# Retiming a hand-written scheduler: longer exponential rounds in the plan, a hold on TensorE, shorter key-value runs

## The chip, the cores and the metric

One core of a Trainium2 chip. The metric is the device time of one execution in microseconds, as the median of several runs. The engines are TensorE (PE; its weight loads are PEld), VectorE (DVE), ScalarE (ACT), GpSimd (POOL) and SyncE (SP).

## The reference

Four residual layers on x of 2048 rows by 512, each on a layer-normed x: A, B, A, B.

```python
def _A_ref(x, wq, wk, wv, wo):          # 32 query heads of 16, one key head, one value head
    q = (x @ wq).reshape(B, S, H, Dh).transpose(0, 2, 1, 3)
    k = x @ wk
    v = x @ wv
    scores = jnp.einsum("bhqd,bkd->bhqk", q, k) * (Dh ** -0.5)
    o = jnp.einsum("bhqk,bkd->bhqd", softmax(scores), v)
    return o.transpose(0, 2, 1, 3).reshape(B, S, H * Dh) @ wo

def _B_ref(x, wqkv, wo):                # linear attention, 32 heads of 16
    q, k, v = ...                       # x @ wqkv, split
    phi = lambda t: jnp.where(t > 0, t + 1, jnp.exp(t)) + 1e-6
    pq, pk = phi(q), phi(k)
    kv = jnp.einsum("bhsd,bhse->bhde", pk, v)
    z = jnp.einsum("bhsd->bhd", pk)
    num = jnp.einsum("bhqd,bhde->bhqe", pq, kv)
    den = jnp.einsum("bhqd,bhd->bhq", pq, z)[..., None] + 1e-6
    return (num / den).transpose(0, 2, 1, 3).reshape(B, S, D) @ wo

for _ in range(2):
    x = x + _A_ref(layernorm(x), A_wq, A_wk, A_wv, A_wo)
    x = x + _B_ref(layernorm(x), B_wqkv, B_wo)
```

## The kernel before

The program's layers are L = 0 to 3; 0 and 2 are softmax attention (`run_a`), 1 and 3 linear attention (`run_b`). The sequence is cut into 16 tiles of 128 rows. In an attention layer a score block is 128 keys by 512 columns (128 queries of 4 heads), so a layer has 4096/2 = 2048 blocks. TensorE makes the scores of several blocks at once in separate row strips (L937); the exponential of a block is made either on ScalarE, 1 to 3 blocks in one ACTIVATE (L1118, a round), or on VectorE, where one eviction to an integer form (L1205) and three shifted copies of up to four blocks (L1247) approximate it. TensorE then sums exponentials times values in column strips into bank 6 (L991), with `V` for ScalarE's blocks and four weighted copies `VW` for VectorE's. PSUM's banks 0 to 5 form two sets of score banks, bases 0 and 3; ScalarE's rounds alternate between them. While one set is read by a round, the other is filled by TensorE.

Nothing of the order on an engine is written out by hand. When the kernel is built, a discrete-event planner (`Planner`) runs generators for all tiles and layers. Each operation has a duration and a latency, given as numbers in the source, and a priority; a free engine takes the ready operation of the best priority (`_dispatch1`). The order so found is written as five fixed instruction streams with semaphore waits (`emit`). The chip keeps these orders and has its own times. The numbers that matter here:

- an exponential round of n blocks lasts 0.051 + 0.4267 n us in the plan (L1118), and its result is there `EX_LAT` = 0.185 later;
- scores take `QK_DUR` = 0.22, are there after `QK_LAT` = 0.438, and a change of TensorE's mode (row strips, column strips, full) costs `SWITCH` = 0.107; scores have priority 0.0, weighted sums 2.0;
- when TensorE has nothing ready, `fill` (L1017 to L1039) issues dummy matmuls of 128 to 512 columns (L1036), as far as a budget allows that grows by `WORK` columns per 3.413 us, and no longer than up to the next expected end of a round (`pl.due`, L1120);
- `soon` (L62) holds an operation back when a better one is about to be ready within `LAG`, but only while `calm`, which is outside the stretches of exponentials;
- `alone` (L1215) gives VectorE a block of its own when its planned backlog is under `DXB`.

In linear layers, `kvt` (layer 3) and `kv_` (layer 1) sum pk times v of a group of 3 or 4 tiles on TensorE, as one operation per bank: 12 or 16 matmuls that the planner treats as one indivisible piece (L1490 to L1502, L1627 to L1636). Most of a linear layer's work is spread among the rounds of the attention layer before or after it; between the last scores of layer 0 and the first of layer 2 lies a short stretch without exponentials, here called the seam.

Of the kernel before, what the change touches and what calls it, by code (L numbers as in the profile page):

```python
# [35 lines left out]
class Planner:  # L36
# [3 lines left out]
    def __init__(self, nc):  # L40
        self.nc = nc
        self.now = 0.0
        self.events = []
        self.seq = 0
        self.ready = {e: [] for e in ENGS}
        self.busy = {e: False for e in ENGS}
        self.until = {e: 0.0 for e in ENGS}
        self.order = {e: [] for e in ENGS}
        self.writer = {}
        self.readers = {}  # L50
        self.flags = {}
        self.flagwait = {}
        self.level = (0.0, 0.0)
        self.due = []
        self.idle = []
        self.mode = None
        self.port = 0.0
        self.calm = False
        self.hungry = []
        self.near = {e: [] for e in ENGS}  # L60

    def soon(self, e, o, dur):  # L62
        lag = {DV: LAG, AC: LAG, PE: LAGP}.get(e)
        if not self.calm or lag is None:
            return 0.0
        n = self.near[e] = [x for x in self.near[e] if x[0] > self.now and x[2].eng is None]
        t = [x[0] for x in n if x[1] + 0.3 < o.prio and x[0] + lag < self.now + dur]
        return min(t) if t else 0.0

    def at(self, t, fn):  # L70
        self.seq += 1
# [68 lines left out]

    def _dispatch(self, e):
        self._dispatch1(e)
        if e == PE and not self.busy[e] and self.idle:
            self.due = [t for t in self.due if t > self.now]
            for f in self.idle:
                f()
        if e == DV and self.hungry and (not self.ready[DV] or self.backlog(DV) < DXB):
            self.hungry[0]()

    def _dispatch1(self, e):  # L150
        if self.busy[e]:
            return
        h = self.ready[e]
        held = []
        while h:
            x = heapq.heappop(h)
            o = x[2]
            if o.eng is not None:
                continue
            dur, fn = o.opts[e]  # L160
            if o.port and self.port > self.now:
                held.append(x)
                continue
            w = self.soon(e, o, dur)
            if w:
                held.append(x)
                self.at(w, lambda: self._dispatch(e))
                break
            if e == PE and STICK and o.mode != "row" and o.mode != self.mode != "row":
                like = [y for y in h if y[2].eng is None and y[2].mode == self.mode and y[0] <= o.prio + STICK]  # L170
                if like:
                    y = min(like)
                    h.remove(y)
                    heapq.heapify(h)
                    held.append(x)
                    o = y[2]
                    dur, fn = o.opts[e]
            if o.port:
                self.port = self.now + dur
            if e == PE:  # L180
                if self.mode != o.mode:
                    dur += max(SWITCH - (self.now - self.until[e]), ROWIN if o.mode == "row" else 0.0)
                self.mode = o.mode
            if e == PE and self.now < COLD:
                dur *= 1.9
            o.eng, o.fn = e, fn
            self.order[e].append(o)
# [190 lines left out]
SWITCH = 0.107  # L378
ROWIN = 0.025
PV_LAT = 0.215  # L380
EX_LAT = 0.185
DH_DUR = 0.22
AH_DUR = 0.28
NBQ = 3
LAG = 0.15
LAGP = 0.05
QLATE = {1: range(4, 14), 3: ()}
PQ = ()
# [1 line left out]
LNEXP = 6  # L390
MCRIT = {0: (), 1: (0, 1), 2: (), 3: ()}
ECRIT = (15,)
WORK = 5000
RING = 24
NOB = 4
DTL = 3.6
# [7 lines left out]
GROW = (5,)  # L404
BLS = 1.6
BLO = 5.0
DXB = 1.6
BLT = 2.5
GA = 3
MW = [None, None, 0, 1, 2, 2, 2, 3, 4, 5, 6, 7, 8, 9, 10, 11]  # L410
# [45 lines left out]
DG = [[0]] + [[t, t + 1] for t in range(1, 15, 2)] + [[15]]  # L456
ACRS = True
EB = "rs"
MCOP = (DV,)*4
EVP = 1.2  # L460
DPP = 1.5
# [7 lines left out]
def bass_interleave_layers__grouped_kv_mqa__linear_attn_block__prompt_kernel(  # L469
# [124 lines left out]
    def B_(i):  # L594
        return ("bank", i)
# [332 lines left out]
    def run_a(L):  # L928
# [111 lines left out]

        pl.idle.append(fill)

        def act_stream():
            if CLM[L]:
                yield ("flag", CLM[L])
# [9 lines left out]
            pl.calm = False  # L1055
            while True:
                s_ = yield ("acq", sets, 0.0)
                group = []
                split = None
                while len(group) < size[s_] and split is None and state["si"] < len(segs):  # L1060
# [54 lines left out]
                if chunk["blk"] and stale():  # L1115
                    dve_close()
                p_ = yield ("acq", pt_pool, 0.0)
                ex = op({AC: (0.051 + 0.4267 * n, lambda e, n=n, s_=s_, p_=p_: e.activation(PT[:, p_, 0:n * 512], ps[:, s_ * 512:(s_ + n) * 512], ACTF.Exp, scale=EXPSC, bias=EXPBIAS))},  # L1118
                        writes=bk + [("PT", p_)], prio=1.0, lat=EX_LAT)
                ex.begun = lambda n=n: pl.due.append(pl.now + 0.051 + 0.4267 * n + 0.17)  # L1120
                pl.give_after(sets, s_, [ex] if split is None else [ex, p1])
                pv_post(ex, [(sg, kt, j, PT[:, p_, i * 512:(i + 1) * 512], ("PT", p_)) for i, (sg, kt, j) in enumerate(group)], [n, [], pt_pool, p_])
            state["done"] = lin["done"] = True
# [76 lines left out]
        def dve_take(extra, own):  # L1200
            sg, kt, j, b = extra
            h, f_ = len(chunk["blk"]), chunk["f"]
            chunk["blk"].append((sg, kt, j))
            dst = FB[:, f_, h * 512:(h + 1) * 512]
            o = op({DV: (0.602, lambda e: e.tensor_scalar(out=dst.bitcast(I16), in0=bank(b), scalar1=VB, scalar2=VLO, op0=ALU.add, op1=ALU.max))},  # L1205
                   writes=[B_(b), ("FB", f_, h)], prio=2.0 if own else 0.5, lat=0.15)
# [164 lines left out]
    def run_b(L):  # L1371
# [93 lines left out]
        def kvt(gi, ts):  # L1465
# [19 lines left out]
            for i, (c, n) in ((1, parts[1]), (0, parts[0])):  # L1485
# [1 line left out]
                    bs[i] = yield ("acq", banks, pr)  # L1487
                b = bs[i]

                def fn(e, i=i, b=b):  # L1490
                    ins = None
                    for g in range(4):
                        for t in ts:
                            if i:
                                ins = e.matmul(ps[:, b * 512 + g:b * 512 + g + 1], lhsT=pk[:, t % 8, g * P:(g + 1) * P], rhs=va[:, t % 8, H * 17 - 1:H * 17],
# [3 lines left out]
                                               start=(not end and t == ts[0]), stop=(t == ts[-1]), skip_group_check=True)  # L1499
                    return ins  # L1500
                rd = [("pk", t % 8) for t in ts] + [("va", t % 8) for t in ts] + [("sacc", u) for u in sorted({2 + t % 8 // 2 for t in ts})]
                op({PE: ((0.04 if i else 0.07) * 4 * len(ts), fn)}, reads=rd, writes=[B_(b)], prio=pr, lat=0.2).cols = (16 if i else 512) * len(ts)  # L1502
                dst = kvacc[:, c:c + n]
                if end:
                    continue
# [94 lines left out]
        def kv_(gi, ts):  # L1600
# [19 lines left out]
            for gs in ((0, 1, 2), (3,)):  # L1620
# [3 lines left out]
                else:  # L1624
                    b = yield ("acq", banks, pr)

                def fn(e, gs=gs, b=b):  # L1627
                    ins = None
                    for i, g in enumerate(gs):
                        for t in ts:  # L1630
                            ins = e.matmul(ps[:, b * 512 + i * 136:b * 512 + (i + 1) * 136], lhsT=pk[:, t % 8, g * P:(g + 1) * P],
                                           rhs=va[:, t % 8, g * 136:(g + 1) * 136], start=(not end and t == ts[0]), stop=(t == ts[-1]), skip_group_check=True)
                    return ins
                rd = [("pk", t % 8) for t in ts] + [("va", t % 8) for t in ts] + [("sacc", u) for u in sorted({2 + t % 8 // 2 for t in ts})]
                o = op({PE: (0.08 * len(gs) * len(ts), fn)}, reads=rd, writes=[B_(b)], prio=pr, lat=0.2)
                o.cols = 136 * len(gs) * len(ts)  # L1636
                dst = kvacc[:, gs[0] * 136:gs[0] * 136 + n]
                if end:
                    continue
# [200 lines left out]
```

## Time and profile before

| | |
|---|---|
| median of 3 runs | 1493.02 us (1491.22 to 1494.28) |
| the profiled execution | 1491.74 us, its span 1490.0 us |
| granted TensorE clock | 0.999 |
| PE busy | 1401.7 us (94%) |
| DVE busy | 1440.6 us (97%) |
| ACT busy | 1455.6 us (98%) |
| exponential rounds (L1118) | 1309, 1399.7 us busy |
| VectorE's evictions (L1205), shifts (L1247) | 1046, 688.9 us; 786, 516.5 us |

A busy engine's records can overlap, so the sum of the means is more than its busy time. A PE that is busy by its records can still be waiting between them.

### The profile page before, as it was taken

How to read it: one execution, taken by the hardware profiler on the slowest of the kernel's cores; microseconds unless marked ns; L12 is line 12 of the kernel's file. 1: busy time of each engine (PE TensorE's matmuls, PEld its weight loads, DVE VectorE, ACT ScalarE, POOL GpSimd, SP SyncE). 2: the span in 40 equal slices, each digit the busy share in tenths (PEclk: the TensorE clock that was granted, in tenths of full speed). 3: DMA queues.
4: the chain of work that ended last, by engine and by line, in shares of the span. 5: the costliest groups of instructions: out<-in, count | busy, mean ns of one | idle time of the engine just before them, and what ended most of it. 6: DMA issues, size and time to landing. Idle time of an engine off the chain costs nothing.

```text
span 1490.0 us, 36100 instructions
## 1 busy us (share of the span) xinstructions
PE 1401.7 (94%) x14660; PEld 511.8 (34%) x14755; DVE 1440.6 (97%) x2684; ACT 1455.6 (98%) x1442; POOL 76.9 (5%) x155
## 2 busy tenths in 40 slices
PE   8999999999999999999999999999999999999998
PEld 4423333322323333323743333333333333333335
DVE  7899999999999999999879999999999999999997
ACT  8999999999999999999799999999999999999996
POOL 5000000000000000000022000000000000000000
PEclk9999999999999999999999999999999999999999
DMA  5100000000000000000031000000000000000001
GB/s 117 71 9 8 9 8 6 8 5 8 9 9 9 9 5 5 2 1 2 2 47 40 2 12 9 12 8 9 4 9 5 9 9 9 8 2 1 2 2 58
DMA packets 53540, 20.71 MB, mean 14 GB/s; under 512 B 47232, under 2 KB 52864, under 8 KB 53376
## 3 DMA queue, kind: packets, MB, share of 16 engines
q1 hardware_dynamic: 52320, 18.36, 5.7%
q8 instruction: 118, 1.93, 0.5%
q14 instruction: 46, 0.38, 0.1%
q10 hardware_dynamic: 1056, 0.03, 0.0%
HBM read 5.28 MB, written 2.10 MB: 5 GB/s over the span
## 4 chain that ended last, share of the span: by engine, by line
DVE 17%; PE 16%; ACT 12%; issue 5%; DMA 1%; ACTq 0%
ACT PT L1118 12%; DVE FB L1205 7%; DVE FB L1247 6%; PE ps L991 5%; PE ps L937 5%; PE ps L683 2%; PE ps L1036 1%; PE ps L851 1%; PE ps L1292 1%; DMA xnT<-xn 1%; DVE sacc L1270 0%; ACT phE L1377 0%; DVE st L765 0%; PE ps L922 0%; DVE QT L1380 0%
## 5 line engine op out<-in xcount | busy, mean ns | idle before, releaser
L1118 ACT ACTIVATE PT<-ps 128x1024 bf16<-128x1024 f32 (+1 forms) x1309 | 1399.7, 1224 | 4.6 <-PE ps L937 3.4
L1205 DVE TENSOR_SCALAR FB<-ps 128x512 int16<-128x512 f32 x1046 | 688.9, 681 | 6.9 <-PE ps L937 4.6
L937 PE MATMUL ps<-QT,KM 32*128 32x512 bf16 x4096 | 530.2, 385 | 36.9 <-ACT PT L1118 23.8
L991 PE MATMUL ps<-FB,VW 128*32 128x512 bf16 x4184 | 527.9, 385 | 17.4 <-ACT PT L1118 6.3
L1247 DVE TENSOR_SCALAR FB<-FB 128x2048 int16<-128x2048 int16 x786 | 516.5, 679 | 0.4
L991 PE MATMUL ps<-PT,V 128*32 128x512 bf16 x3050 | 482.8, 386 | 13.4 <-ACT PT L1118 9.9
L937 PEld LDWEIGHTS ps<-QT,KM 32*128 32x128 bf16 x4096 | 133.0, 91 | 433.7 <-ACT PT L1118 301.2
L991 PEld LDWEIGHTS ps<-FB,VW 128*32 128x32 bf16 x4184 | 131.8, 94 | 184.4 <-issue 83.5
L1036 PE MATMUL ps<-QT,V 128*32 128x512 bf16 (+6 forms) x758 | 178.4, 312 | 1.6 <-DVE FB L1205 1.6
L991 PEld LDWEIGHTS ps<-PT,V 128*32 128x32 bf16 x3050 | 120.6, 94 | 128.6 <-issue 59.9
L1036 PEld LDWEIGHTS ps<-QT,V 128*32 128x32 bf16 x758 | 60.0, 95 | 81.5 <-issue 52.0
L756 POOL TENSOR_TENSOR rs<-ve,mhalf 128x1 f32<-128x1 f32 x59 | 43.5, 738 | 579.7 <-DVE ve L754 576.6
L683 PE MATMUL ps<-wqkv,xnT 128*128 128x512 bf16 (+1 forms) x220 | 62.8, 367 | 5.7 <-issue 3.2
L754 POOL TENSOR_SCALAR ve<-mv 128x1 f32<-128x1 f32 x32 | 14.1, 439 | 674.3 <-DVE mv L766 674.1
L1377 ACT ACTIVATE phE<-ps 128x512 bf16<-128x512 f32 (+1 forms) x66 | 42.0, 638 | 6.2 <-PE ps L851 4.6
L1292 PE MATMUL ps<-identF,sacc 128*128 128x128 f32 x256 | 46.8, 291 | 0.8 <-DVE sacc L1270 0.8
L1270 DVE COPY sacc<-ps 128x512 f32<-128x512 f32 x64 | 43.6, 681 | 1.3 <-PE ps L991 1.1
L765 DVE BATCH_NORM_STATS2 st<-x_sb 128x6 f32<-128x512 bf16 x60 | 40.6, 681 | 2.2 <-DMA x_sb<-in_A_x_dram 2.0
L851 PE MATMUL ps<-xnT,wqkv 128*128 128x128 bf16 x512 | 38.8, 220 | 0.0
L851 PE MATMUL ps<-xnT,wq 128*128 128x128 bf16 x464 | 36.3, 220 | 0.9 <-DVE FB L1205 0.4
L1292 PEld LDWEIGHTS ps<-identF,sacc 128*128 128x128 f32 x256 | 27.4, 140 | 22.2 <-issue 13.5
L851 PEld LDWEIGHTS ps<-xnT,wqkv 128*128 128x128 bf16 x512 | 29.7, 98 | 10.0 <-issue 6.6
(139 smaller groups left out, 630.9 us busy)
## 6 DMA issues: line engine op xcount, KB each, us to landing
out_dram<-x_sb SPq DMA_DIRECT2D x16, 128.0 KB, 1.7
x_sb<-in_A_x_dram SPq DMA_DIRECT2D x6, 256.0 KB, 4.4
wqkv<-in_B_wqkv_dram SPq DMA_DIRECT2D x1, 1536.0 KB, 8.8
xnT<-xn SPq DMA_TRANSPOSE x48, 2.4
x_sb<-in_A_x_dram SPq DMA_DIRECT2D x4, 128.0 KB, 2.2
wq<-in_A_wq_dram SPq DMA_DIRECT2D x1, 512.0 KB, 4.2
wo<-in_A_wo_dram SPq DMA_DIRECT2D x1, 512.0 KB, 4.0
wo<-in_B_wo_dram SPq DMA_DIRECT2D x1, 512.0 KB, 9.6
```

The source lines that it names most:

```text
L683: return e.matmul(dst, lhsT=l, rhs=r, start=(k == 0), stop=(k == len(pairs) - 1))
L756: op({PO: (0.55, lambda e: e.tensor_tensor(out=rs[:, t:t + 1], in0=ve[:, t:t + 1], in1=mhalf[:], op=ALU.pow))}, reads=[("ve", t), "mhalf"] ...
L851: ins = e.matmul(dst[:, g * P:(g + 1) * P], lhsT=lhs(g, k), rhs=rhs(k), start=(k == 0), stop=(k == FT - 1))
L937: return e.matmul(bank(b), lhsT=KM[r, sg.par, kt * P:(kt + 1) * P], rhs=QT[r, sg.t, :], start=True, stop=True)
L991: ins = e.matmul(ps[32 * j:32 * j + 32, ACC * 512:(ACC + 1) * 512], lhsT=V[:, kt, :] if w is None else VW[:, kt, w, :], rhs=ap, start=(k = ...
L1036: o = op({PE: (n / 2400.0, lambda e: e.matmul(ps[32 * j:32 * j + 32, b * 512:b * 512 + n], lhsT=V0[:], rhs=QT[:, sg.t, 0:n], start=st, sto ...
L1118: ex = op({AC: (0.051 + 0.4267 * n, lambda e, n=n, s_=s_, p_=p_: e.activation(PT[:, p_, 0:n * 512], ps[:, s_ * 512:(s_ + n) * 512], ACTF.E ...
L1205: o = op({DV: (0.602, lambda e: e.tensor_scalar(out=dst.bitcast(I16), in0=bank(b), scalar1=VB, scalar2=VLO, op0=ALU.add, op1=ALU.max))}, w ...
L1247: o = op({en: (du, lambda e, w=w, g_=g_: e.tensor_scalar(out=FB[:, g_, 0:n].bitcast(I16), in0=FB[:, f_, 0:n].bitcast(I16), scalar1=float(w ...
L1270: o = op({DV: (0.6, lambda e, src=src: e.tensor_copy(src, bank(ACC)))}, writes=[B_(ACC), key], prio=0.0, lat=0.15)
L1292: o = op({PE: (0.12, lambda e, c=c: e.transpose(ps[:, b * 512 + c * P:b * 512 + (c + 1) * P], src[:, c * P:(c + 1) * P], identF[:]))}, rea ...
L1377: op({AC: (0.07 + n / 1200.0, lambda e: e.activation(phE[:, i, 0:n], bank(b, n), ACTF.Exp))}, reads=[B_(b)], writes=[("phE", i)], prio=pr ...
```

## The change

Four edits to the planner and the recording of operations. The arithmetic is the same.

1. An exponential round lasts `EXO` + 0.4267 n in the plan, with EXO = 0.0625, less up to `EXI` = 0.03 when ScalarE was idle before it; the expected end that bounds the fillers follows from it.
2. At the start of each round a *turn* is noted: the time at which the round's set of banks will be free, and the latest start of scores with which the other set's round is followed without a break. When TensorE is about to start an operation that isn't scores and isn't a filler, `yields` looks whether that operation would end too late for a turn within 0.2 us; if so the operation is held until the set is free. While something is held (`keep`), no filler is started either. The same holds for operations held by `soon`.
3. The key-value sums are recorded as one operation per 128-column group, 3 or 4 matmuls each, in `kvt` and in `kv_`.
4. Constants: LAG 0.15 to 0.18, WORK 5000 to 5500, DXB 1.6 to 1.4.

```diff
+        self.turns = []
+        self.keep = 0.0
...
+    def yields(self, dur):
+        self.turns = [x for x in self.turns if x[0]() > self.now - 0.004]
+        for rel, late in self.turns:
+            r = rel()
+            if r < self.now + HMAX and self.now + dur - max(r, late()) > HTOL + HK * max(0.0, r - self.now):
+                return max(r, self.now) + 0.005
+        return 0.0
...
     def _dispatch(self, e):
         self._dispatch1(e)
-        if e == PE and not self.busy[e] and self.idle:
+        if e == PE and not self.busy[e] and self.idle and self.now >= self.keep:
...
             w = self.soon(e, o, dur)
             if w:
+                if e == PE:
+                    self.keep = w
                 held.append(x)
...
+            if e == PE and o.mode != "row" and o.prio < 9.0:
+                w = self.yields(dur + (max(0.0, SWITCH - (self.now - self.until[e])) if self.mode != o.mode else 0.0))
+                if w:
+                    self.keep = w
+                    held.append(x if x[2] is o else y)
+                    self.at(w, lambda: self._dispatch(e))
+                    break
...
+            if e == AC and o.mode == "exp":
+                dur -= min(EXI, self.now - self.until[e])
...
+EXO = 0.0625
+EXI = 0.03
-LAG = 0.15
+LAG = 0.18
-WORK = 5000
+WORK = 5500
-DXB = 1.6
+DXB = 1.4
+OWNP = 2.0
+HMAX = 0.2
+KSP = True
+HTOL = 0.02
+HK = 0.3
...
+        rounds, ex_ = {}, {}
...
                 s_ = yield ("acq", sets, 0.0)
+                if s_ in rounds and rounds[s_][2] in pl.turns:
+                    pl.turns.remove(rounds[s_][2])
...
-                ex = op({AC: (0.051 + 0.4267 * n, lambda e, ...: e.activation(...))}, ..., prio=1.0, lat=EX_LAT)
-                ex.begun = lambda n=n: pl.due.append(pl.now + 0.051 + 0.4267 * n + 0.17)
+                ex = op({AC: (EXO + 0.4267 * n, lambda e, ...: e.activation(...))}, ..., prio=1.0, lat=EX_LAT, mode="exp")
+                def begun(n=n, s_=s_, p1=p1 if split is not None else None):
+                    e1 = pl.until[AC]
+                    pl.due.append(e1 + 0.17)
+                    nx = rounds.get(3 - s_)
+                    d = nx[1] if nx and nx[0].eng is None else EXO + 0.8534
+                    turn = (lambda: max(e1 + EX_LAT, 0.0 if p1 is None else p1.end or p1.due or 1e9), lambda: e1 + d - QK_LAT - SWITCH)
+                    pl.turns.append(turn)
+                    rounds[s_] = (ex_[s_], 0.0, turn)
+                ex_[s_] = ex
+                rounds[s_] = (ex, EXO + 0.4267 * n, None)
+                ex.begun = begun
...
-                   writes=[B_(b), ("FB", f_, h)], prio=2.0 if own else 0.5, lat=0.15)
+                   writes=[B_(b), ("FB", f_, h)], prio=OWNP if own else 0.5, lat=0.15)
...
-                def fn(e, i=i, b=b):
+                def fn(e, gs, i=i, b=b):
                     ins = None
-                    for g in range(4):
+                    for g in gs:
...
-                op({PE: ((0.04 if i else 0.07) * 4 * len(ts), fn)}, reads=rd, writes=[B_(b)], prio=pr, lat=0.2).cols = (16 if i else 512) * len(ts)
+                for gs in (((0, 1, 2, 3),) if i or not KSP else ((0,), (1,), (2,), (3,))):
+                    op({PE: ((0.04 if i else 0.07) * len(gs) * len(ts), lambda e, gs=gs, fn=fn: fn(e, gs))}, reads=rd, writes=[B_(b)], prio=pr, lat=0.2).cols = (4 if i else 128) * len(gs) * len(ts)
...
-                def fn(e, gs=gs, b=b):
-                    ins = None
-                    for i, g in enumerate(gs):
+                for i, g in enumerate(gs):
+                    def fn(e, i=i, g=g, b=b):
+                        ins = None
                         for t in ts:
...
-                o = op({PE: (0.08 * len(gs) * len(ts), fn)}, reads=rd, writes=[B_(b)], prio=pr, lat=0.2)
-                o.cols = 136 * len(gs) * len(ts)
+                    op({PE: (0.08 * len(ts), fn)}, reads=rd, writes=[B_(b)], prio=pr, lat=0.2).cols = 136 * len(ts)
```

More of the change, by code (lines that the diff above doesn't have):

```diff
@@ L1117, in act_stream @@
                 p_ = yield ("acq", pt_pool, 0.0)
-                ex = op({AC: (0.051 + 0.4267 * n, lambda e, n=n, s_=s_, p_=p_: e.activation(PT[:, p_, 0:n * 512], ps[:, s_ * 512:(s_ + n) * 512], ACTF.Exp, scale=EXPSC, bias=EXPBIAS))},
-                        writes=bk + [("PT", p_)], prio=1.0, lat=EX_LAT)
-                ex.begun = lambda n=n: pl.due.append(pl.now + 0.051 + 0.4267 * n + 0.17)
+                ex = op({AC: (EXO + 0.4267 * n, lambda e, n=n, s_=s_, p_=p_: e.activation(PT[:, p_, 0:n * 512], ps[:, s_ * 512:(s_ + n) * 512], ACTF.Exp, scale=EXPSC, bias=EXPBIAS))},
+                        writes=bk + [("PT", p_)], prio=1.0, lat=EX_LAT, mode="exp")
+                def begun(n=n, s_=s_, p1=p1 if split is not None else None):
[9 more added lines that the diff above has]
+                ex.begun = begun
                 pl.give_after(sets, s_, [ex] if split is None else [ex, p1])
@@ L1625, in kv_ @@
                     b = yield ("acq", banks, pr)
-                def fn(e, gs=gs, b=b):
-                    ins = None
-                    for i, g in enumerate(gs):
+                rd = [("pk", t % 8) for t in ts] + [("va", t % 8) for t in ts] + [("sacc", u) for u in sorted({2 + t % 8 // 2 for t in ts})]
+                for i, g in enumerate(gs):
+                    def fn(e, i=i, g=g, b=b):
+                        ins = None
                         for t in ts:
@@ L1632, in fn @@
                                            rhs=va[:, t % 8, g * 136:(g + 1) * 136], start=(not end and t == ts[0]), stop=(t == ts[-1]), skip_group_check=True)
-                    return ins
-                rd = [("pk", t % 8) for t in ts] + [("va", t % 8) for t in ts] + [("sacc", u) for u in sorted({2 + t % 8 // 2 for t in ts})]
-                o = op({PE: (0.08 * len(gs) * len(ts), fn)}, reads=rd, writes=[B_(b)], prio=pr, lat=0.2)
-                o.cols = 136 * len(gs) * len(ts)
+                        return ins
+                    op({PE: (0.08 * len(ts), fn)}, reads=rd, writes=[B_(b)], prio=pr, lat=0.2).cols = 136 * len(ts)
                 dst = kvacc[:, gs[0] * 136:gs[0] * 136 + n]
```

## The prediction

> **What bounds the kernel now.** I read the page's totals first, then the busy time by stage, the groups of instructions by shape, the waits, and the chain of work around the seam between the layers.
>
> ```profile
> span 1490.0 us, 36100 instructions
> PE 1401.7 (94%) x14660; PEld 511.8 (34%) x14755; DVE 1440.6 (97%) x2684; ACT 1455.6 (98%) x1442; POOL 76.9 (5%) x155
> ```
>
> Three engines are nearly full, so the shares alone don't name the bound. The stages do (columns: stretch, length, then busy us of PE, weight loads, DVE, ACT, POOL; granted clock; DMA).
>
> ```profile
> 0.00:50.00 50.00, 45.24 (x465) 23.88 (x467) 37.61 (x110) 43.53 (x48) 22.24 (x71) 0.97 0.52 138
> ...
> 700.00:750.00 50.00, 48.04 (x605) 31.85 (x604) 42.65 (x109) 39.12 (x62) 2.30 (x5) 1.00 0.02 4
> ...
> 1450.00:1490.00 40.00, 35.93 (x363) 22.89 (x363) 29.57 (x66) 25.91 (x36) 0.00 (x0) 0.99 0.16 54
> ...
> 55.00:705.00 650.00, 613.43 (x6344) 202.91 (x6384) 645.04 (x1150) 648.68 (x619) 19.86 (x23) 1.00 0.03 6
> 755.00:1450.00 695.00, 654.06 (x6841) 227.35 (x6885) 682.48 (x1247) 693.68 (x677) 32.14 (x55) 1.00 0.05 10
> ```
>
> In the two long attention stretches ScalarE (ACT) stands still for 650 - 648.68 = 1.32 and 695 - 693.68 = 1.32 us: 2.6 us of 1345. It is the bound there, VectorE close behind with 4.96 + 12.52 = 17.5 us idle. The rest of ACT's idle time is at the start (6.5 us), the seam between the two attention layers (10.9 us) and the end (14.1 us). So the time can be written as ACT's work plus ACT's idle time, and the change is worth what it does to these two.
>
> ```profile
> L1118 ACT ACTIVATE PT<-ps 128x1024 bf16<-128x1024 f32 x875 | 861.2, 1086 | 2.3 <-PE ps L937 1.9
> ...
> L1118 ACT ACTIVATE PT<-ps 128x1536 bf16<-128x1536 f32 x433 | 628.2, 1505 | 2.3 <-PE ps L937 1.5
> ...
> L1118 ACT ACTIVATE PT<-ps 128x512 bf16<-128x512 f32 x1 | 0.7, 668 | 0.0
> ...
> ACT PT L1118 <- PE ps L937: 3.4, 12, 0.5
> ...
> PEld ps L937 <- ACT PT L1118: 301.2, 789, 1.3
> ...
> PEld ps L991 <- ACT PT L1118: 71.3, 169, 1.2
> ```
>
> An exponential round (L1118) handles 2 or 3 score blocks. It had to wait visibly for its scores 12 times, 3.4 us in all; the scores' weight load (L937) waited for a round to end 789 times, 301 us in all. TensorE is normally there first and waits for ACT, about 0.38 us each time.
>
> **The round's duration.** The plan's round is 0.051 + 0.4267 per block: 0.904 and 1.331 us; after the change 0.0625 back to back: 0.916 and 1.343. Which fits? The records overlap, so I count rounds in a stretch in which ACT hardly stops, 800 to 1450:
>
> ```profile
> L1118 ACT ACTIVATE PT<-ps 128x1024 bf16<-128x1024 f32 x424 | 415.5, 1090 | 0.6 <-PE ps L937 0.5
> L1118 ACT ACTIVATE PT<-ps 128x1536 bf16<-128x1536 f32 x182 | 264.4, 1506 | 0.0
> L1377 ACT ACTIVATE phE<-ps 128x512 bf16<-128x512 f32 x29 | 19.6, 677 | 0.0
> L839 ACT ACTIVATE KM<-ps,kmask 128x512 bf16<-128x512 f32 x1 | 0.7, 735 | 0.0
> L1441 ACT CAST va<-ps 128x512 bf16<-128x512 f32 x1 | 0.7, 692 | 0.0
> ```
>
> With the old values, and 0.497 us (the plan's) for each phE and 1.3 for the last two rows, this makes 424 x 0.904 + 182 x 1.331 + 14.4 + 1.3 = 641.4 of 650 us, 8.6 short. With the new ones 388.4 + 244.4 + 14.4 + 1.3 = 648.5, 1.5 short; a round cut off at the edge can hide up to 1.3 more. So the new duration is the chip's, to within 2.8 us / 606 = 5 ns a round, and what is left over, 1.5 to 2.8 us in 650, is all the waiting of ACT there. Over 1345 us: 3.1 to 5.8 us. This is the most that a better order can take from the two stretches.
>
> The Trainium skill, "ScalarE: Activation LUTs", section "What ACT_TABLE_LOAD costs", has an ACTIVATE with immediate scale and bias at 186 ns + 0.833 ns an element, less about 93 ns back to back: an estimate of 946 ns for 1024 elements. By it the new plan would still be 30 ns a round too short, 39 us in 1309 rounds. The count above leaves no room for that, and the sum goes by the count.
>
> **The change part by part.** The order of each engine's instructions can be counted in both built programs. The work hardly moves.
>
> ACT's rounds: 875, 433 and 1 (of 2, 3 and 1 blocks) become 878, 431 and 0: 3 x 1.086 - 2 x 1.505 - 0.668 = -0.42 us. The first layer gives 1513 -> 1510 blocks to ACT, the second 1537 -> 1539. VectorE gets one block more.
>
> ```profile
> L1205 DVE TENSOR_SCALAR FB<-ps 128x512 int16<-128x512 f32 x1046 | 688.9, 681 | 6.9 <-PE ps L937 4.6
> ...
> L1247 DVE TENSOR_SCALAR FB<-FB 128x2048 int16<-128x2048 int16 x780 | 513.3, 680 | 0.4
> ...
> L839 ACT ACTIVATE KM<-ps,kmask 128x128 bf16<-128x128 f32 x4 | 1.5, 366 | 1.5 <-PE ps L683 1.4
> ...
> L839 ACT ACTIVATE KM<-ps,kmask 128x256 bf16<-128x256 f32 x1 | 0.5, 474 | 0.1
> ...
> L839 ACT ACTIVATE KM<-ps,kmask 128x512 bf16<-128x512 f32 x2 | 1.4, 712 | 0.1
> ...
> L840 DVE TENSOR_SCALAR KM<-ps,kmask 128x128 bf16<-128x128 f32 x4 | 1.4, 344 | 0.0
> ```
>
> VectorE: one eviction more (L1205, 0.68), three full shifts fewer (L1247), three of 1536 and three of 1024 more, which cost at most as much: between -1 and +3 us spread over 1345, and 17.5 us of idle time hide it.
>
> The key copies (KM) that may go to either engine: ACT does one of 512 more early in the first layer (+0.71), one of 512 and one of 256 fewer in the second (-0.71 - 0.47), three of 128 more in the seam, where it has idle time. On the path: -0.47. Together ACT's work changes by -0.9 us.
>
> ACT's waits. In the old plan TensorE starts whatever is ready, up to a run of 12 or 16 key-value matmuls as one piece:
>
> ```profile
> L1631 PE MATMUL ps<-va,sacc 128*128 128x136 bf16 x64 | 5.3, 224 | 0.2 <-DVE kvacc L1641 0.2
> ...
> L1498 PE MATMUL ps<-sacc,va 128*128 128x128 bf16 x64 | 4.4, 220 | 0.0
> ```
>
> 12 x 5.3/64 = 1.0 us and 16 x 4.4/64 = 1.1 us, longer than a 2-block round, so scores queued behind one come late. The change cuts them to pieces of 4 (0.33 and 0.28 us) between which scores fit; the number of matmuls stays. In the built order the stretches between two score groups that hold over 0.9 us of other needed columns (weighted sums counted four abreast, fillers left out) fall from 37 to 28 (over 1.1 us: 7 to 4). The hold (`yields`) stops ordinary work that would make the next scores late. What it holds back is delayed by 0.2 us at most, and is covered by the 301 us that TensorE waits anyway. Of the 3.1 to 5.8 us of waits I take 2.5 as saved, by the ratio 28/37 for the long stretches and a little more for the hold; the ends are a gain of 5.8 and no gain.
>
> Fillers. WORK, 5000 -> 5500 columns, and the longer rounds let in more dummy matmuls: 758 -> 927, with 255 -> 670 of the full 512 columns; 258,368 -> 399,488 columns.
>
> ```profile
> L1036 PE MATMUL ps<-QT,V 128*32 128x512 bf16 x255 | 86.4, 385 | 1.4 <-DVE FB L1205 1.4
> ...
> L1036 PE MATMUL ps<-QT,V 128*32 128x128 bf16 x121 | 24.0, 221 | 0.0
> ```
>
> (385 - 221) / 384 columns = 0.43 ns a column, so 141,120 more columns are 60 us of TensorE. They lie in its 301 us of waiting for ACT; I cost them at nothing. The granted clock is 1.00 already, so they can't earn anything. If the cover is gone, they cost what the first rival says.
>
> The seam. Between the last scores of the first layer and the first of the second, VectorE's order loses the three 128-wide key writes (3 x 0.344 = 1.03 us) to ACT, and some layer-norm pieces. The chain there runs along VectorE (columns: start, length, what):
>
> ```profile
> 734.28 0.54 DVE QT L1380
> 734.83 0.60 DVE va L1743
> 735.42 0.01 DVE KM L840
> ...
> 735.66 0.40 DVE phE L1378
> 736.09 0.69 DVE QT L1380
> 736.78 0.33 DVE QT L698
> ...
> 737.34 0.70 DVE QT L1380
> ...
> 738.09 0.41 PE ps L937 x3
> ...
> 738.53 3.72 ACT PT L1118 x3
> ```
>
> Only one key write shows in it, so I take 0.7 of the 1.03 us; the ends are -2 and +2, since LAG (0.15 -> 0.18) reorders this stage as a whole. The start and the end keep their instructions; DMAs are 116 on SyncE in both, in nearly the same order. At zero, with +-1.
>
> Sum: -0.9 - 2.5 - 0.7 = -4.1 us. The profiled execution took 1491.74 (span 1490.0), 1.3 under the median, so 1487.6 for a profiled one, and 1493.0 - 4.1 = 1488.9 for the median.
>
> **The rivals.**
>
> (A) The margin is eaten, slower. A plan that thought ACT faster than it is put TensorE's scores early; that is why ACT waits so little. The exact duration puts them just in time, the 60 us of fillers take 60/789 = 0.076 us of each of the 789 waits, and any lateness of VectorE then passes through TensorE to ACT. A hold also keeps back all that is queued behind it: weighted sums (L991), which free the exponentials' buffers. It decides once about one round in ten (130 of 1309) starts 0.1 us late: 13 us, less the 0.9 of work: 1505. For it: 60 of 301 us is a real cut, and the fillers' median grows. Against: at 0.38 us the mean wait remains 0.3 us, and the hold plans for just this case. The Trainium skill, "TensorE: Matmul & The Clock Gate", Part 2, says that only weight loads are pulled ahead and "The MATMULs themselves stay in program order"; that agrees with the 169 times that L991's loads stood waiting for a round, and it is this rival's premise.
>
> (B) Nothing moves: the waits saved come back elsewhere (VectorE, 17.5 us from full, sets the pace). Only work and seam remain: -0.9 to +1, 1492.5.
>
> (C) More than the waits: the seam and the start gain 2 us each beside the waits: -0.9 - 4 - 4 = -8.9, 1484.
>
> **How the numbers follow.** About 0.2%, 3 us, is what a measurement of this kernel can tell from no change. Forecast 0.52 (1485 to 1492; about 0.1 of it within 3 us of the old time), A 0.25 (1496 to 1506), B 0.13, C 0.10. Faster by over 0.2%: 0.42 + 0.10 = 0.52. Slower: A, 0.25. Same: 0.10 + 0.13 = 0.23. The range leaves out the half of C below 1484 and the part of A above 1499: 1484 to 1499. The forecast's own range is 1485 to 1492.
>
> **What would show it.** Right: the visible wait of L1118 for L937 falls from 3.4 us, ACT's idle time in the two stretches stays under 2.6 us; the scores' 301 us of waiting falls by about 60; the first long run of rounds of the second layer begins about 1 us before 738.5. Wrong: ACT busy falls below 99.5% in the stretches, the waits of L1118 for L937 rise in number, or ACT waits for buffers; for C, the seam's 10.9 us shrinks by over 2.

## The result, and the profile after

The changed kernel takes 1487.66 us (8 runs, 1487.22 to 1489.33) against 1492.74 (8 runs): 5.1 us less, a ratio of 0.9967 with a 95% interval of 0.9956 to 0.9978. Its profiled execution took 1489.33 us with a span of 1487.6, so the two profiles differ by 2.4 us only. Line numbers move: rounds L1118 -> L1150, scores L937 -> L965, weighted sums L991 -> L1019, evictions L1205 -> L1247.

The page and the stages of the changed kernel (columns as before):

```profile
span 1487.6 us, 36547 instructions
...
PE 1433.2 (96%) x14825; PEld 520.1 (35%) x14924; DVE 1439.2 (97%) x2686; ACT 1452.5 (98%) x1444; POOL 77.0 (5%) x155
```

```profile
0.00:50.00 50.00, 45.08 (x484) 24.62 (x491) 40.64 (x115) 43.89 (x49) 21.85 (x71) 1.00 0.53 139
700.00:750.00 50.00, 49.22 (x615) 32.32 (x613) 41.52 (x107) 39.38 (x65) 2.69 (x6) 1.00 0.02 5
...
55.00:705.00 650.00, 628.22 (x6432) 206.08 (x6474) 646.68 (x1157) 649.23 (x624) 21.28 (x23) 1.00 0.03 6
755.00:1450.00 695.00, 672.72 (x6937) 232.90 (x6982) 681.66 (x1248) 692.00 (x675) 31.18 (x55) 1.00 0.06 10
```

In the first stretch ACT's idle time falls from 1.32 to 0.77 us; in the second it rises from 1.32 to 3.00. Part of that rise is this one execution's: the granted clock dropped just there (a_cap384 below, with the same order and no such drop there, has 2.17).

```profile
750.00:757.00 7.00, 6.37 (x40) 2.13 (x41) 3.73 (x8) 6.35 (x7) 0.79 (x2) 0.76 0.27 56
757.00:764.00 7.00, 7.00 (x61) 2.47 (x60) 6.19 (x15) 6.19 (x6) 2.07 (x6) 1.00 0.19 37
```

A mean of 0.76 over 7 us is a clock of one half for 3.4 us. ACT's rounds stopped three times around it (start, length, what, idle time before):

```profile
736.46 18.18 ACT L1150 ACTIVATE PT<-ps 128x1536 bf16<-128x1536 f32 x16 [0.50 <-PE ps L965]
755.29 2.36 ACT L1150 ACTIVATE PT<-ps 128x1536 bf16<-128x1536 f32 x2 [0.65 <-PE ps L965]
757.88 1.45 ACT L1150 ACTIVATE PT<-ps 128x1536 bf16<-128x1536 f32 x1 [0.22 <-PE ps L965]
759.92 12.32 ACT L1150 ACTIVATE PT<-ps 128x1024 bf16<-128x1024 f32 x11 [0.59 <-PE ps L1019]
```

The first long run of rounds of the second attention layer starts at 736.46 instead of 738.53. The rounds and the waits:

```profile
L1150 ACT ACTIVATE PT<-ps 128x1024 bf16<-128x1024 f32 x878 | 888.5, 1171 | 2.1 <-PE ps L965 0.9 <-PE ps L1019 0.9
...
L1150 ACT ACTIVATE PT<-ps 128x1536 bf16<-128x1536 f32 x431 | 651.1, 1588 | 3.5 <-PE ps L1019 1.8 <-PE ps L965 1.7
```

```profile
PEld ps L965 <- ACT PT L1150: 381.7, 1023, 1.2
...
PEld ps L1019 <- ACT PT L1150: 4.9, 12, 0.7
...
ACT PT L1150 <- PE ps L1019: 2.7, 4, 1.3
...
ACT PT L1150 <- PE ps L965: 2.6, 6, 0.7
```

Two things stand out. The scores' loads now wait for a round 1023 times (789 before), the weighted sums' loads 12 times (169 before). A round's end frees both: the set of banks for the next scores and the exponentials for the weighted sums. Before, the sums often stood first in TensorE's queue, with the scores behind them; now the scores stand first. The third row shows a price: four rounds now wait 2.7 us for weighted sums (L1019), which must have read a buffer of exponentials before a round may write it again; before, no such wait was visible. And the record of a 2-block round is longer, 1171 ns against 1086: a record begins while the round ahead is still running, so a longer one means that its scores had come earlier.

The views don't show short waits, because they vanish in the overlap of the records. I measured them from the records' ends: the end of a round less the end of ACT's instruction before it. Most rounds stand at 0.916 (2 blocks) and 1.343 us (3 blocks), the middle half within 1 to 2 ns; what exceeds this is wait, and a wait over 0.03 us counts as one piece. The two stretches of rounds then split into the rounds' own time, waits, and ACT's other instructions between them (us, profiled executions):

| kernel | median | rounds' own | waits (pieces) | other on ACT | seam | tail |
|---|---|---|---|---|---|---|
| before | 1492.74 | 1383.5 | 10.5 (46) | 27.2 | 24.5 | 35.1 |
| changed | 1487.66 | 1383.1 | 7.7 (20) | 28.2 | 24.2 | 34.7 |
| a_cap384 | 1487.43 | 1383.1 | 5.8 (13) | 28.3 | 24.2 | 34.7 |
| a_near | 1486.12 | 1385.8 | 3.8 (14) | 24.4 | 26.0 | 35.0 |
| a_near2 | 1495.65 | 1383.5 | 8.7 (22) | 36.5 | 24.3 | 34.8 |
| a_oldround | 1494.71 | 1389.1 | 6.1 (18) | 28.0 | 24.9 | 36.8 |
| a_longkv | 1491.38 | 1383.5 | 10.1 (35) | 29.5 | 24.4 | 34.8 |
| a_oldconst | 1492.25 | 1382.7 | 6.2 (26) | 30.3 | 24.5 | 36.7 |
| a_nohold | 1490.95 | 1383.2 | 8.3 (52) | 28.4 | 24.4 | 35.2 |
| a_fill64 | 1508.92 | 1383.1 | 24.2 (52) | 28.1 | 24.2 | 34.7 |
| b_hold | 1498.86 | 1389.4 | 7.0 (21) | 33.4 | 22.9 | 34.9 |
| b_newround | 1494.54 | 1377.7 | 15.3 (80) | 30.5 | 24.9 | 34.9 |
| b_near | 1496.01 | 1383.0 | 11.7 (42) | 30.2 | 24.7 | 34.8 |
| b_fill512 | 1508.73 | 1383.5 | 27.7 (137) | 27.2 | 24.5 | 35.1 |

The columns, the start (9 us) and a rest of 0.3 us at most add up to the span. In seven of these profiles the granted clock was halved for a while inside the stretches, and some of the waits stand there (up to 10 us after its end): 0.8 us before, 1.8 changed, 4.0 in a_near2, 2.8 in a_oldround, 1.7 in a_longkv, 1.4 in b_hold and 18.5 in a_fill64.

What the rounds waited for can be read off as well. In 43 of the 46 pieces of the kernel before, 8.0 us, the round starts some 154 ns after the end of its last score matmul (between 148 and 162), so it was the scores that were late; in one, 0.2 us, it was a weighted sum. In the changed kernel late scores make 15 pieces and 3.6 us, weighted sums four pieces and 3.1 us. Of the pieces before, 22 (3.4 us) had weighted sums right ahead of the scores on TensorE, four (0.8 us) a key-value run.

Of the 2.4 us between the two profiles, 2.7 are waits, 0.4 the rounds, 0.3 and 0.4 seam and tail; 1.1 us more of other instructions and 0.3 of a later start go the other way.

### The profile page after: what moved, and what is told of

Read it like the earlier page. It is cut to its first block, busy times and chain, and to the rows that moved or that the text cites. A ratio compares the mean times of both kernels' runs of the same rounds, so it can differ in the third digit from the quotient of the medians.

```text
span 1487.6 us, 36547 instructions
## 1 busy us (share of the span) xinstructions
PE 1433.2 (96%) x14825; PEld 520.1 (35%) x14924; DVE 1439.2 (97%) x2686; ACT 1452.5 (98%) x1444; POOL 77.0 (5%) x155
## 4 chain that ended last, share of the span: by engine, by line
DVE 46%; PE 38%; ACT 7%; issue 7%; DMA 1%; POOL 0%; POOLq 0%; SPq 0%; ACTq 0%
DVE FB L1247 22%; DVE FB L1289 16%; PE ps L1019 13%; PE ps L965 11%; ACT PT L1150 7%; PE ps L711 5%; PE ps L1064 4%; PE ps L879 2%; PE ps L1334 1%; DVE sacc L1312 1%; DVE st L793 1%; DVE xn L802 1%; DVE QT L1422 1%; DVE Osb L1345 1%; DVE sacc L1422 1%
## 5 line engine op out<-in xcount | busy, mean ns | idle before, releaser
L1150 ACT ACTIVATE PT<-ps 128x1024 bf16<-128x1024 f32 (+1 forms) x1309 | 1400.1, 1309 | 5.6 <-PE ps L1019 2.7
L1247 DVE TENSOR_SCALAR FB<-ps 128x512 int16<-128x512 f32 x1047 | 689.0, 680 | 4.4 <-PE ps L965 3.1
L965 PE MATMUL ps<-QT,KM 32*128 32x512 bf16 x4096 | 525.6, 385 | 24.9 <-ACT PT L1150 16.9
L1019 PE MATMUL ps<-FB,VW 128*32 128x512 bf16 x4188 | 526.1, 384 | 8.3 <-DVE sacc L1312 5.3
L1289 DVE TENSOR_SCALAR FB<-FB 128x2048 int16<-128x2048 int16 (+1 forms) x789 | 517.6, 676 | 0.3
L1019 PE MATMUL ps<-PT,V 128*32 128x512 bf16 x3049 | 472.8, 386 | 0.4 <-issue 0.3
L965 PEld LDWEIGHTS ps<-QT,KM 32*128 32x128 bf16 x4096 | 133.0, 91 | 466.5 <-ACT PT L1150 381.7
L1064 PE MATMUL ps<-QT,V 128*32 128x512 bf16 (+6 forms) x927 | 249.8, 347 | 0.4
L1019 PEld LDWEIGHTS ps<-FB,VW 128*32 128x32 bf16 x4188 | 130.4, 94 | 163.3 <-issue 97.1
L1019 PEld LDWEIGHTS ps<-PT,V 128*32 128x32 bf16 x3049 | 114.7, 94 | 102.9 <-issue 74.5
L1064 PEld LDWEIGHTS ps<-QT,V 128*32 128x32 bf16 x927 | 79.8, 96 | 88.6 <-issue 32.9
L1419 ACT ACTIVATE phE<-ps 128x512 bf16<-128x512 f32 (+1 forms) x66 | 45.8, 696 | 6.0 <-PE ps L879 5.0
L879 PE MATMUL ps<-xnT,wq 128*128 128x128 bf16 x464 | 35.2, 220 | 0.0
L879 PEld LDWEIGHTS ps<-xnT,wqkv 128*128 128x128 bf16 x512 | 29.5, 98 | 9.8 <-issue 7.0
```

The lines of the kernel that those rows point to most:

```text
L879: ins = e.matmul(dst[:, g * P:(g + 1) * P], lhsT=lhs(g, k), rhs=rhs(k), start=(k == 0), stop=(k == FT - 1))
L965: return e.matmul(bank(b), lhsT=KM[r, sg.par, kt * P:(kt + 1) * P], rhs=QT[r, sg.t, :], start=True, stop=True)
L1019: ins = e.matmul(ps[32 * j:32 * j + 32, ACC * 512:(ACC + 1) * 512], lhsT=V[:, kt, :] if w is None else VW[:, kt, w, :], rhs=ap, start=(k = ...
L1064: o = op({PE: (n / 2400.0, lambda e: e.matmul(ps[32 * j:32 * j + 32, b * 512:b * 512 + n], lhsT=V0[:], rhs=QT[:, sg.t, 0:n], start=st, sto ...
L1150: ex = op({AC: (EXO + 0.4267 * n, lambda e, n=n, s_=s_, p_=p_: e.activation(PT[:, p_, 0:n * 512], ps[:, s_ * 512:(s_ + n) * 512], ACTF.Exp ...
L1289: o = op({en: (du, lambda e, w=w, g_=g_: e.tensor_scalar(out=FB[:, g_, 0:n].bitcast(I16), in0=FB[:, f_, 0:n].bitcast(I16), scalar1=float(w ...
```

## The experiments

Each ran in five rounds beside the kernel before. Names with a_ are edits of the changed kernel, with b_ of the one before.

**The same orders with other fillers.** Three kernels keep every engine's order and change only the columns of the dummy matmuls.

```diff
b_fill512 (from the kernel before)
-  e.matmul(ps[..., b * 512:b * 512 + n], lhsT=V0[:], rhs=QT[:, sg.t, 0:n], ...)
+  e.matmul(ps[..., b * 512:b * 512 + 512], lhsT=V0[:], rhs=QT[:, sg.t, 0:512], ...)
a_fill64 (from the changed kernel): 64 columns instead of n
a_cap384 (from the changed kernel): min(n, 384) columns
```

> The order of the kernel before, instruction for instruction; only each of its 758 dummy matmuls now has 512 columns (258,368 -> 388,096 columns, about as many as the change has; +55 us of TensorE at 0.43 ns a column). Fillers are covered (the prediction's sum): 1492.7 +- 1.5, and the visible wait of L1118 for L937 stays near 3.4 us, while L937's 301 us of waiting for rounds falls by some 50. The margin is eaten (rival A): scores come late in a share of the rounds; ACT's idle time in the two stretches grows by 2 us or more, 1495 or above.

1508.73 us, ratio 1.0098 (1.0066 to 1.0131), 16 us slower. The waits of the rounds for their scores:

```profile
PEld ps L937 <- ACT PT L1118: 283.1, 726, 1.3
...
ACT PT L1118 <- PE ps L937: 9.4, 32, 0.6
```

The visible waits rise from 12 to 32, the counted ones from 46 pieces and 10.5 us to 137 and 27.7. These 17.2 us are the whole difference. TensorE still waits 283 us for rounds, so that sum is no cover. In 83 of the pieces a filler had run since the scores before (13 in the kernel before), though only 8 have one directly ahead of the late scores, and 87 have weighted sums there. So the fillers seem to cost mostly by delaying the work queued behind them, and the scores after that. Rival A's mechanism is real, at 17.2 us for 55 us of fillers.

> The order of the changed kernel, instruction for instruction; only its 927 dummy matmuls have 64 columns each (399,488 -> 59,328; -145 us of TensorE). Fillers are covered and buy nothing: 1487.7 +- 1.5, same clock. The margin is eaten: scores come earlier and the time falls by 2 us or more, 1485.7 or below. Fillers hold the granted clock up: the clock row falls below 0.99 and the time rises by several us.

1508.92 us, ratio 1.0119 (1.0072 to 1.0165). The third expectation held. TensorE's clock halves 13 times inside the span, for 3.4 or 6.8 us; one such place:

```profile
325.00:336.00 11.00, 9.46 (x75) 2.73 (x75) 9.09 (x17) 9.03 (x9) 0.00 (x0) 0.69 0.01 2
336.00:347.00 11.00, 10.80 (x126) 3.31 (x123) 10.85 (x20) 10.89 (x11) 0.00 (x0) 1.00 0.06 13
```

ACT's waits are 24.2 us in 52 pieces, and 37 of these, 18.5 us, stand in a halving or within 10 us of its end. Each of the 13 halvings follows on 3.4 us in which TensorE is busy only 61 to 73% by the records; about half of all other such stretches are 95% busy or more, and 16 of 417 are as low without a halving behind them. So the fillers do earn something: they keep the clock. The Trainium skill, "TensorE: Matmul & The Clock Gate", Part 1, says that the gate knows two states, full and half, and judges windows of 3.4 us; the lengths 3.4 and 6.8 us and the half clock agree. It has the clock drop after an idle window, though, and here the windows ahead were 61 to 73% busy.

> The order of the changed kernel, instruction for instruction, with its dummy matmuls cut off at 384 columns (399,488 -> 312,576 columns, -37 us of TensorE). Fillers that the plan has placed are covered: 1487.5 +- 0.7 in runs at full clock. They still take margin, as the 512-column ones did in the order of before (+55 us of TensorE, +17 us of ACT's waits): 1 us or more faster at full clock. They keep the clock up: more runs with a clock under 0.999 than the 2 of 8 of the changed kernel, and a median above 1488.5.

1487.43 us, ratio 0.9963 (0.9949 to 0.9978): the same as the changed kernel. At full clock 1487.2 (4 of 6 runs) against 1487.6 (6 of 8). So 37 us of the changed kernel's fillers cost some 0.3 us: where the plan has placed them, this much of them is covered. Nor do these few runs show that a fifth of the columns is needed for the clock.

**The hold.**

```diff
a_nohold (from the changed kernel)
-                w = self.yields(dur + ...)
+                w = 0.0
```

> The changed kernel with the hold (yields) answering 0 always; 1311 rounds of 3049 blocks on ScalarE, the same blocks as with it. The hold carries the saved waits: 1489.5 to 1490.5, with the short waits of ACT back (waits of L1150 for L965 nearer the 12 of before). The exact duration and shorter runs carry them: 1487.7 +- 1. A plan's luck decides: anything within 3 us of either, with the difference at one or two places of the trace.

1490.95 us, ratio 0.9981 (0.9960 to 1.0001): 3.3 us over the changed kernel, 0.5 above the first expectation, with 52 pieces of wait instead of 20. The visible waits for scores did not come back (4, where the changed kernel has 6); most of the 52 are too short to be visible. The waits at the end of a round are shared as in the kernel before, with the weighted sums' loads back from 12 to 192:

```profile
PEld ps L965 <- ACT PT L1150: 298.6, 793, 1.4
PEld ps L1019 <- ACT PT L1150: 57.7, 192, 0.6
```

The 2-block rounds' records show it at a glance:

```profile
L1150 ACT ACTIVATE PT<-ps 128x1024 bf16<-128x1024 f32 x882 | 863.4, 1081 | 1.0 <-PE ps L1019 0.4 <-PE ps L965 0.2
```

The mean is 1081 ns, as before the change. In all fourteen kernels this number goes with the hold: 1071 to 1086 without it, 1158 to 1199 with it. In microseconds the hold is worth less than the pieces suggest: 8.3 us of waits without it against 5.8 in a_cap384 with it.

> The kernel before with the hold alone: old duration of a round, long key-value runs, LAG 0.15, WORK 5000, DXB 1.6. 3064 blocks in 1308 rounds on ScalarE: +14 x 0.427 - 0.06 = +5.9 us of work. The hold saves waits in any plan: ACT's waits in the two stretches fall from 10.5 us to 5 to 7, and the time is 1492.7 + 5.9 - 4.5 = 1494. The hold needs the exact duration: waits stay at 10 us, 1498.

It undoes everything but the hold: the constants and the duration at their old values, long key-value runs. 1498.86 us, ratio 1.0042 (1.0026 to 1.0057): slower than before, above the 1494 expected.

```profile
L1150 ACT ACTIVATE PT<-ps 128x1024 bf16<-128x1024 f32 x856 | 871.6, 1187 | 3.6 <-PE ps L1019 1.6 <-PE ps L965 1.6
```

The hold does its work here too (1187 ns; the weighted sums' loads wait 7 times; 21 pieces, 7.0 us, 1.4 of them around a halved clock, so 3.5 us or more of waits saved), but the plan gives ScalarE 14 blocks more (+5.9 us), and ACT's other instructions take 6.2 us more, which I hadn't expected. So the hold alone is no gain in this plan, which divides the work in another way.

**The duration.**

```diff
a_oldround (from the changed kernel): EXO = 0.051, EXI = 0.0
b_newround (from the kernel before), the same two places:
-  0.051 + 0.4267 * n
+  0.0625 + 0.4267 * n
```

> The changed kernel with the old duration of a round in the plan (EXO 0.051, EXI 0). Its plan gives ScalarE 3062 blocks in 1316 rounds, 13 blocks and 7 rounds more. ACT's work plus idle time is the time: +13 x 0.427 + 7 x 0.06 = +6 us of work, 1493.5, if its waits stay as in the changed kernel. If the old duration is a margin that spares waits (rival A's premise), less: about 1491. If the plan is only luck: within 1485 to 1491.

1494.71 us, ratio 0.9999 (0.9978 to 1.0021). Waits 6.1 us in 18 pieces, of which 2.8 us in 5 pieces stand around a halved clock of 6.8 us in this profile. That leaves 3.3 us, less than the 5.8 of a_cap384 and near the 3.8 of a_near below, whose duration is the longest. So whether the short duration is a margin that spares waits isn't settled once the hold is there; 2.5 us is the most that these plans leave for it. The 13 extra blocks cost 6.0 us, as expected; the tail is 2.1 us longer.

> The kernel before with the new duration of a round alone (0.0625 + 0.4267 n, in the plan and in the fillers' bound). Its plan gives ScalarE 3037 blocks in 1305 rounds (3050 in 1309 before): -13 x 0.427 - 4 x 0.06 = -5.8 us of ACT's work; VectorE gets 13 blocks more, 13 x (0.68 + 0.75 x 0.68) = +15.5 us, of its 17.5 us idle in the two stretches. If ACT's work plus waits is still the time and the waits stay: 1487. If VectorE is then the bound, its lateness passes to ACT as waits and the time stays at 1490 to 1494. Without the hold, an exact duration also takes the margin (rival A's premise): ACT's short waits rise over the 47 of before, 1490 or more.

1494.54 us, ratio 1.0002 (0.9988 to 1.0015). Here what the rival foretold shows: 5.8 us less work on ACT, but 80 pieces of wait for 46, and 15.3 us for 10.5; other instructions take 3.3 us more. VectorE, the other candidate, doesn't look like the cause: it is idle for 17.0 us in the two windows of the stages (17.5 before), and TensorE never stood still for over 0.1 us ahead of the late scores.

```profile
L1118 ACT ACTIVATE PT<-ps 128x1024 bf16<-128x1024 f32 x874 | 857.9, 1076 | 3.2 <-PE ps L937 2.3
```

In these two plans the exact duration moves work to VectorE and loses the gain again in waits, and the hold saves waits and loses them again in work; the changed kernel has both and loses neither. That the two belong together in every plan isn't shown: a_nohold has the exact duration without the hold too, and waits only 8.3 us.

**Constants and key-value runs.**

```diff
a_oldconst (from the changed kernel): LAG = 0.15, WORK = 5000, DXB = 1.6
a_longkv (from the changed kernel): KSP = False, and kv_ records one operation for all its groups again
```

> The changed kernel with LAG 0.15, WORK 5000 and DXB 1.6; 3049 blocks in 1303 rounds, fillers 816 of 263,872 columns in all (927 of 399,488). ACT's work is 0.4 us less. Fillers are neutral as long as the plan places them: 1487.5 +- 1.5, clock 1.00. If the extra fillers are what keeps the clock up (their cut to 64 columns took the mean clock to 0.98): clock under 0.998 and 1490 or more.

1492.25 us, ratio 0.9989 (0.9976 to 1.0002). Waits and work are the changed kernel's; the tail is 2.0 us longer and other instructions 2.0 us. Neither expectation named that.

> The changed kernel with the key-value sums as runs of 12 and 16 matmuls again; 3050 blocks in 1308 rounds, +0.4 us of work. The short runs save waits of their own: 1490 or more, with waits of ACT behind key-value runs. The hold does it without them (a long run is held until the set is free): 1488 +- 1.

1491.38 us, ratio 0.9986 (0.9973 to 1.0000). Waits rise to 10.1 us in 35 pieces (1.7 us in 4 pieces around a halved clock); 3 of the pieces, 0.9 us, stand right behind key-value runs of layer 3, and 19, 5.7 us, have weighted sums right ahead of their scores. So this plan waits more, but little of the 3.7 us can be put down to the long runs themselves.

**Neighbours.** How far do plans scatter that differ by 1 ns in the duration of a round?

```diff
a_near (from the changed kernel): EXO = 0.0635      a_near2: EXO = 0.0615
b_near (from the kernel before): 0.052 + 0.4267 * n
```

> A neighbour of the changed kernel, EXO 0.0635 instead of 0.0625, to see how far the time scatters between plans that mean the same. 3055 blocks in 1312 rounds: 6 x 0.427 + 3 x 0.06 = +2.7 us of ACT's work. Work plus waits: 1490.4 +- 1. If plans scatter by luck beyond their work: outside 1488 to 1493.

> The other neighbour of the changed kernel, EXO 0.0615; 3050 blocks in 1308 rounds, +0.4 us of work. If the changed kernel is an ordinary one of its kind: 1486 to 1489, waits in the two stretches 4 to 8 us in some 20 pieces. If plans scatter by more than what the change brings: outside 1484 to 1491.

> A neighbour of the kernel before: 0.052 for 0.051 in the duration of a round; 3049 blocks in 1307 rounds, 0.5 us less work. If the kernel before is an ordinary one of its kind: 1490 to 1493 (1491 at full clock), with about 10 us of waits in the two stretches, 40 or more of them. If plans scatter by more than what the change brings: outside 1488 to 1495.

1486.12 (ratio 0.9953, 0.9935 to 0.9971), 1495.65 (1.0023, 1.0013 to 1.0033) and 1496.01 us (1.0023, 1.0010 to 1.0036). All three fall where the expectations had put a scatter beyond the counted work; a_near is the fastest kernel of the study, though its interval and the changed kernel's overlap. The waits of rounds keep their kind (14 and 22 pieces with the hold, 6 of the 22 around a halved clock; 42 without). What scatters is ACT's other instructions: 24.4, 36.5 and 30.2 us. In a_near2 one instruction makes 5.6 us of it:

```profile
ACT xnT L705 <- PE ps L822: 5.6, 1, 5.6
```

```profile
745.85 2.50 ACT L1150 ACTIVATE PT<-ps 128x1536 bf16<-128x1536 f32 x2
753.96 0.59 ACT L705 COPY xnT<-ps 128x512 bf16<-128x512 bf16 x1 [5.60 <-PE ps L822]
755.43 0.17 ACT L705 CAST V<-ps 128x16 bf16<-128x16 f32 x1 [0.89 <-PE ps L711]
756.31 0.98 ACT L867 ACTIVATE KM<-ps,kmask 128x256 bf16<-128x256 f32 x2 [0.70 <-PE ps L711]
757.31 1.45 ACT L1150 ACTIVATE PT<-ps 128x1536 bf16<-128x1536 f32 x1
```

A copy that may go to either engine (`copy_flex`) went to ScalarE, ahead of the next round. It needs a transpose on TensorE, and this needs a normed row tile (xn), which VectorE wrote only then:

```profile
752.40 0.40 DVE L802 TENSOR_SCALAR xn<-x_sb,mv,rs 128x512 bf16<-128x512 bf16 x1
```

```profile
753.53 0.39 PE L822 MATMUL ps<-ident,xn 128*128 128x128 bf16 x4
```

Between the two lie 0.7 us of TensorE's queue; the rest of the 5.6 us is the wait for the layer norm. The order on ACT is fixed by the plan, so no round started for 9.0 us, from the end of the second one at 748.35 to 757.31. In b_near a phE of layer 1 did the same in a smaller way, 6.7 us where the kernel before has 4.6:

```profile
ACT phE L1377 <- PE ps L851: 6.7, 6, 2.6
```

## Why the prediction was right or wrong

The forecast, 1488.9 us and faster, was right: 1487.66, 5.1 us less for the 4.1 forecast. Between runs with a granted clock of 1.000 the gain is 3.4 us; the other 1.7 went with the clock, which the prediction had at no gain. That the sum came so near was partly luck: the same kind of count missed a_near by 4.3 us and b_hold by 4.9, and the ranges given for b_near and a_near2 by 3.0 and 6.7.

*The bound* held as far as it was tried: ACT's rounds and other instructions fill 1410.7 of the 1421.2 us of the two stretches before, and 13 more blocks cost the counted 6.0 us (a_oldround). The 13 fewer of b_newround gained nothing, because waits and other instructions grew by more. That the columns of the table add up is so by construction.

*The duration* held: back-to-back rounds stand at 0.916 and 1.343 us. The estimate of 946 ns from the Trainium skill, "ScalarE: Activation LUTs", section "What ACT_TABLE_LOAD costs", isn't borne out by any run here.

*ACT's work*, forecast -0.9 us, is the term that was mis-sized: the rounds gave the counted -0.4, but the other instructions in the two stretches took 1.1 us more, not 0.5 less. I had counted the key copies alone; two more phE of the linear layers had moved from the seam into the stretches (49 -> 51, 0.49 us each).

*The waits*, forecast -2.5, came out a little larger: -2.7 with a clock dip in the second stretch of the changed kernel's profile, -4.7 by a_cap384, which has the same order and no dip inside the stretches (0.8 us of the waits before stand around a dip at 28 us, so -3.9 may be nearer). The limit of 3.1 to 5.8 us was too low: the kernel before waits 10.5 us. The prediction had spread its count of the stretch from 800 to 1450 over everything; there the records' ends give 2.9 us, but 7.5 us stand ahead of it. The reason was only partly mine. I looked for long runs in front of the scores; most of it was the weighted sums standing ahead of the scores (169 -> 12 waits), which the hold turned round. What the hold keeps back isn't free either: four rounds wait 3.1 us for weighted sums, which was one of the prediction's signs of being wrong and rival A's second point. Of the signs of being right, the visible wait for scores fell (12 to 6 waits, 3.4 to 2.6 us) and the second layer's long run began earlier, by 2.1 us. But ACT's idle time in the two stretches did not stay under 2.6 us (3.8; 2.9 in a_cap384), and that the scores' 301 us of waiting would fall by 60 was wrong: they rose to 382.

*The seam*, -0.7 forecast, gave -0.3, and the start of the rounds came 0.3 later; the tail, put at zero, gave -0.4.

*The fillers* at nothing: right in amount as far as it was tried (0.3 us for 37 of the 60, a_cap384), wrong in both reasons. TensorE's waiting time is no cover (b_fill512), and fillers earn the clock (a_fill64).

*Rival A* is a real mechanism that befell this kernel only in the 3.1 us of waits for weighted sums: it struck b_fill512, at 17.2 us and 91 further pieces of wait, near the 13 us and 130 rounds of its price, and b_newround, by 4.8 us. The prediction's reason against it was the hold; a_nohold, without it, has 52 pieces but only 8.3 us of waits, so the hold is not all that kept the rival away. *Rival B* fell: the waits didn't come back. *Rival C* was too much for this plan.

What the prediction did not see is the scatter. A plan 1 ns away lies 8.0 us above the changed kernel, another 1.5 below. And a_near2, with all four edits, is slower than the kernel before. So that these edits make such a kernel faster isn't shown beyond this one plan: a forecast from the meaning of the edits alone could not have told 1486 from 1496, and the counts of blocks and rounds couldn't either, because what scattered was ACT's other instructions. For the same reason the single removals (+3.3 to +7.0 us) are no shares of the 5.1: only what shows in a kernel's own trace, such as the 20 pieces of wait for 52, is shown to belong to the edit.

## What to carry to other kernels

When one engine is the bound, write the time as its own work, its waits and its other instructions, each from the records' ends, and compare plans by these three: a plan's constants act on all of them at once. Where the order on an engine is fixed when the program is built, put the work that feeds the bound ahead of work that becomes ready at the same event. Before removing one part of a scheduler's change to price it, run a neighbour that means the same, to learn what a difference must exceed.

## What the runs showed of the hardware

TensorE's granted clock halved for 3.4 or 6.8 us at a time even in profiles in which it is 94 to 97% busy by the records (the kernel before, the changed one, a_longkv, a_oldround, a_near2), and another execution of the same program has more or fewer of these dips: the kernel before had clocks from 0.989 to 1.000 in 23 runs. The time of a run follows its granted clock: the kernel before took 1490.7 to 1491.8 us in the 7 of 23 runs with 1.000, 1493.9 to 1495.8 in the 4 with 0.997 and 1502.0 to 1503.9 in the 5 with 0.989 or 0.990, some 1.1 us for each thousandth. At 1.000 the changed kernel takes 1487.6 (6 of 8 runs), so about 3.4 of the 5.1 us between the medians are the order's, by the middle of those 7 runs (1491.0); the rest goes with fewer dips. That the changed kernel's larger fillers are the cause of that is not shown: b_fill512, with about as many columns in the old order, still dipped in 2 of 6 runs, and b_newround stood at 1.000 in all 12 of its runs.

A round's own time, from the end of ACT's instruction before it, is 0.916 us for 1024 columns and 1.343 us for 1536, with the middle half of some 1300 rounds within 2 ns in every kernel here.
